# A layer norm, state-space scan and gated MLP kernel: 512-token chunks, 64-row matmul pairs for the half tiles, input constant moved to C

## Chip, cores, metric

The kernel runs on one core of a Trainium2 chip. The metric is device time in microseconds, taken from runs of the whole program; a run's profile gives its own, slightly shorter span. Engines in the profile are PE (TensorE), PEld (TensorE weight loads), DVE (VectorE), ACT (ScalarE), POOL (GpSimd) and SP (SyncE, which here issues DMAs). "L404" is line 404 of the kernel that was profiled. The granted clock is the share of TensorE's full clock that the trace records, 1.00 being full. An evacuation is the copy of a matmul's result out of TensorE's result memory.

## The reference, cut to what matters

Input x is 2048 tokens by 448 features, bf16. F is 1792, the state has 448 complex channels.

```python
xn = layernorm(x)
Lam_bar = exp(dt * Lam);  B_bar = ((Lam_bar - 1) / Lam)[:, None] * Bmat       # complex, 448 x 448
h[t] = Lam_bar * h[t-1] + B_bar @ xn[t]                                     # 2048 steps
s = 2 * Re(h @ Cmat.T) + xn * Dskip
z = (sigmoid(xn @ w_gate) * (xn @ w_up)) @ w_down
out = x + s * silu(z)
```

448 is three and a half times 128, so every contraction over features has three full 128-row tiles and a half one of 64 rows.

## The kernel before

Tokens go in eight chunks of 256. Each chunk is layer-normed and transposed, goes through gate/up (`gu`), hidden product (`hF`) and down projection, and through the state part: input projection (`bu`), rotation of each channel by its phase, a real scan over time on VectorE (one instruction for the real and one for the imaginary part), rotation back, output projection (`y`). The half tile is padded with zeros to a full one: four matmuls for each contraction of 448.

```python
TC = 256; NCH = 8; KT = 4; PT = 4
...
def emit_ffn(c, xnT):
    for ft in range(FT):                                  # 14 tiles of F
        gu = ps.tile([P, 2, TC], FP32, name="gu", bufs=2)
        for cc, wmat in enumerate((wg, wu)):
            for kt in range(KT):                          # 4 full matmuls, the last half zeros
                nc.tensor.matmul(gu[:, cc, :], lhsT=wmat[:, kt, ft * P:(ft + 1) * P], rhs=xnT[:, kt, :], ...)
        if len(pending) >= DOWN_LAG:
            down_mms(*pending.pop(0))                     # down projection of the same chunk, 4 tiles behind
        ...
        nc.vector.tensor_tensor(out=hF[:], in0=sig[:], in1=ub[:], op=ALU.mult)
...
def emit_ssm(c, xnT, K):
    for pt in range(PT):                                  # 4 tiles of state channels
        ...                                               # bu = B_bar^T xn: 8 matmuls, copied to bus by ScalarE
        nc.vector.tensor_tensor(out=ta[:], in0=bus[:], in1=cosb, op=ALU.mult)
        ...                                               # tb, z
        nc.vector.tensor_tensor_scan(out=wv[:, 0, :], data0=rb, data1=z[:, 0, :], ...)
        nc.vector.tensor_tensor_scan(out=wv[:, 1, :], data0=rb, data1=z[:, 1, :], ...)
        ...                                               # tc, td, hT; 4 matmuls into y
```

The layer norm's subtraction ran on ScalarE and its square root was ScalarE's. The scheduler of the compiler chose the order within each engine.

## Time and profile before

| | before |
|---|---|
| time, median of 3 runs | 254.73 us (254.04 to 256.77) |
| span of the profiled run | 252.6 us |
| PE, DVE, ACT busy | 84%, 83%, 59% |
| period of one 256-token chunk in the middle | 24.43 us |

The first lines of the profile's page of before: the busy time of each engine with its share of the span, and the busy tenths in 40 slices of 6.3 us each.

```profile
span 252.6 us, 4548 instructions
PE 212.4 (84%) x1616; PEld 155.4 (62%) x1616; DVE 209.0 (83%) x624; ACT 149.0 (59%) x362; POOL 5.6 (2%) x14
PE   0065996388898949999999999999999799999990
DVE  4699798699999996999789978988899799286324
```

The reader sees two engines with the same share. The slices tell them apart: from the sixteenth on PE shows nines but for one seven and the end, so TensorE sets the middle of the kernel, and the loss is in the first 100 us. Stretches of 20 us of before, with busy time and instruction count of PE, PEld, DVE, ACT and POOL, then the granted TensorE clock, the busy share of the DMA engines and the GB/s that they moved:

```profile
80.00:100.00 20.00, 15.41 (x88) 8.57 (x86) 17.86 (x57) 10.99 (x28) 0.00 (x0) 0.83 0.11 21
100.00:120.00 20.00, 19.96 (x167) 16.03 (x164) 19.33 (x58) 12.11 (x34) 0.00 (x0) 1.00 0.04 13
140.00:160.00 20.00, 19.83 (x155) 14.71 (x152) 17.45 (x51) 11.68 (x31) 0.00 (x0) 1.00 0.12 27
```

From 100 to 180 us TensorE has hardly a gap (19.8 to 20.0 of each 20 us). In that stage only less TensorE work, or faster, can help.

### The profile page before, as it was taken

The numbers are of one execution on the slowest core, as the hardware profiler recorded it, in microseconds if no ns is written. First come the engines' busy times: TensorE is split into PE (matmuls) and PEld (weight loads), VectorE is DVE, ScalarE is ACT, GpSimd is POOL, SyncE is SP. The second block draws the span as 40 slices with busy tenths as digits, with TensorE's granted clock in tenths as the row PEclk, the third lists the DMA queues.
The fourth block names the chain that finished last, engine by engine and source line by source line (L and its number), as shares of the span: only waits on it lengthen the run. The fifth ranks groups of instructions, "written<-read, shape, count | busy, mean of one in ns | idle before, by whom it ended". The sixth has DMA issues, their size and how long they took to land.

```text
span 252.6 us, 4548 instructions
## 1 busy us (share of the span) xinstructions
PE 212.4 (84%) x1616; PEld 155.4 (62%) x1616; DVE 209.0 (83%) x624; ACT 149.0 (59%) x362; POOL 5.6 (2%) x14
## 2 busy tenths in 40 slices
PE   0065996388898949999999999999999799999990
PEld 0043974275487704887688668867888377756750
DVE  4699798699999996999789978988899799286324
ACT  6595999965564527665565566547656465453331
POOL 8000000000000000000000000000000000000000
PEclk9998899799999976999999999999999999999997
DMA  6999930000211002100210021011100010001001
GB/s 215 207 301 324 313 13 3 0 0 0 25 36 21 3 0 43 38 3 0 42 39 0 3 42 36 3 22 21 39 1 3 0 35 4 0 0 40 0 0 39
DMA packets 15863, 12.07 MB, mean 48 GB/s; under 512 B 7232, under 2 KB 14912, under 8 KB 15840
## 3 DMA queue, kind: packets, MB, share of 16 engines
q1 hardware_dynamic: 15600, 11.67, 18.0%
q0 software_dynamic: 240, 0.12, 0.7%
q8 instruction: 12, 0.20, 0.3%
q14 instruction: 11, 0.09, 0.1%
HBM read 8.37 MB, written 1.84 MB: 40 GB/s over the span
## 4 chain that ended last, share of the span: by engine, by line
PE 47%; DVE 29%; ACT 10%; DMA 9%; issue 4%; SPq 1%; ACTq 0%; DVEq 0%
PE gu L390 22%; DMA wu<-in_B_w_up_dram 6%; DVE wv L352 5%; DVE wv L354 5%; PE bu L329 5%; DVE hF L404 3%; DMA b_im<-in_A_B_im_dram 3%; DVE tb L347 3%; DVE z L349 2%; DVE ta L345 2%; DVE td L366 2%; ACT bus L334 1%; ACT ct_350 L256 1%; DVE tc L364 1%; PE dacc_2979 L382 1%
## 5 line engine op out<-in xcount | busy, mean ns | idle before, releaser
L390 PE MATMUL gu<-xnT,wg 128*128 128x256 bf16 x448 | 71.4, 276 | 9.2 <-ACT ub L403 8.5
L390 PE MATMUL gu<-xnT,wu 128*128 128x256 bf16 x448 | 74.9, 276 | 1.2 <-DMA wu<-in_B_w_up_dram 1.2
L397 ACT ACTIVATE sig<-gu 128x256 bf16<-128x256 f32 x112 | 43.1, 385 | 51.2 <-PE gu L390 51.0
L390 PEld LDWEIGHTS <-wg 128*128 128x128 bf16 x448 | 44.1, 99 | 24.0 <-issue 9.9
L390 PEld LDWEIGHTS <-wu 128*128 128x128 bf16 x448 | 44.2, 99 | 7.2 <-DMA wu<-in_B_w_up_dram 1.7
L329 PE MATMUL bu<-xnT,bbarT 128*128 128x256 bf16 x256 | 46.5, 275 | 0.9 <-ACT bus L334 0.8
L403 ACT CAST ub<-gu 128x256 bf16<-128x256 f32 x98 | 36.2, 370 | 0.0
L382 PEld LDWEIGHTS <-hF 128*128 128x128 bf16 x224 | 20.7, 98 | 21.1 <-DVE hF L404 14.6
L329 PEld LDWEIGHTS <-bbarT 128*128 128x128 bf16 x256 | 25.2, 99 | 8.6 <-issue 2.9
L404 DVE TENSOR_TENSOR hF<-sig,ub 128x256 bf16<-128x256 bf16 x98 | 26.3, 280 | 4.6 <-ACT ub L403 4.4
L334 ACT CAST bus<-bu 128x512 bf16<-128x512 f32 x32 | 18.7, 590 | 12.1 <-ACT ub L403 4.7
L371 PEld LDWEIGHTS <-hT 128*128 128x128 bf16 x128 | 12.9, 102 | 13.5 <-issue 2.6
L305 ACT ACTIVATE xm<-x_all,nmean 128x448 bf16<-128x448 bf16 x16 | 9.8, 673 | 12.2 <-DVE xn L306 7.7
L345 DVE TENSOR_TENSOR ta<-bus,cosT 128x512 bf16<-128x512 bf16 x32 | 13.2, 415 | 3.9 <-ACT cosT L294 2.0
L426 DVE TENSOR_TENSOR g_t<-zb,sigd 128x448 bf16<-128x448 bf16 x16 | 6.2, 386 | 10.5 <-ACT zb L413 10.5
L368 DVE TENSOR_TENSOR hT<-tc,td 128x512 bf16<-128x512 bf16 x32 | 12.9, 416 | 1.7 <-PE y_1143 L371 1.6
L347 DVE TENSOR_TENSOR tb<-bus,spm 128x512 bf16<-128x512 bf16 x32 | 13.2, 413 | 1.2 <-ACT spm L290 1.2
L349 DVE TENSOR_TENSOR z<-ta,tb 128x512 bf16<-128x512 bf16 x32 | 13.4, 420 | 0.4
L364 DVE TENSOR_TENSOR tc<-wv,cosT 128x512 bf16<-128x512 bf16 x32 | 13.4, 419 | 0.2
L366 DVE TENSOR_TENSOR td<-wv,spm 128x512 bf16<-128x512 bf16 x32 | 13.4, 417 | 0.0
L400 DVE TENSOR_TENSOR hF<-sig,gu 128x256 bf16<-128x256 bf16 x14 | 5.9, 419 | 8.4 <-ACT sig L397 8.4
L313 PE MATMUL tpx<-ident,xn 128*128 128x128 bf16 x16 | 2.1, 311 | 12.5 <-DVE xn L306 12.4
(238 smaller groups left out, 338.7 us busy)
## 6 DMA issues: line engine op xcount, KB each, us to landing
out_dram<-o_t SPq DMA_DIRECT2D x16, 112.0 KB, 1.9
wd<-in_B_w_down_dram SPq DMA_DIRECT2D x1, 1568.0 KB, 9.1
wg<-in_B_w_gate_dram SPq DMA_DIRECT2D x1, 1344.0 KB, 11.2
wu<-in_B_w_up_dram SPq DMA_DIRECT2D x1, 1344.0 KB, 15.1
x_all<-in_A_x_dram SPq DMA_DIRECT2D x1, 1120.0 KB, 11.6
x_all<-in_A_x_dram SPq DMA_DIRECT2D x1, 672.0 KB, 4.4
c_re<-in_A_C_re_dram SPq DMA_DIRECT2D x1, 336.0 KB, 15.9
c_im<-in_A_C_im_dram SPq DMA_DIRECT2D x1, 336.0 KB, 16.2
```

The source lines that it names most:

```text
L329: nc.tensor.matmul(bu[:, cc, :], lhsT=K["bbarT"][:, kt, cc, pt * P:(pt + 1) * P], rhs=xnT[:, kt, :], start=(kt == 0), stop=(kt == KT - 1))
L334: nc.scalar.copy(out=bus[:], in_=bu[:])
L345: nc.vector.tensor_tensor(out=ta[:], in0=bus[:], in1=cosb, op=ALU.mult)
L347: nc.vector.tensor_tensor(out=tb[:], in0=swap_pair(bus[:]), in1=spm_v, op=ALU.mult)
L349: nc.vector.tensor_tensor(out=z[:], in0=ta[:], in1=tb[:], op=ALU.add)
L364: nc.vector.tensor_tensor(out=tc_[:], in0=wv[:], in1=cosb, op=ALU.mult)
L366: nc.vector.tensor_tensor(out=td[:], in0=swap_pair(wv[:]), in1=smp_v, op=ALU.mult)
L382: nc.tensor.matmul(dacc[j][:, :], lhsT=hF[:, j * P:(j + 1) * P], rhs=wd[:, ft, :], start=(ft == 0), stop=(ft == FT - 1))
L390: nc.tensor.matmul(gu[:, cc, :], lhsT=wmat[:, kt, ft * P:(ft + 1) * P], rhs=xnT[:, kt, :], start=(kt == 0), stop=(kt == KT - 1))
L397: nc.scalar.activation(sig[:], gu[:, 0, :], ACT.Sigmoid)
L403: nc.scalar.copy(out=ub[:], in_=gu[:, 1, :])
L404: nc.vector.tensor_tensor(out=hF[:], in0=sig[:], in1=ub[:], op=ALU.mult)
```

## The change

Its intent: give TensorE less to do. The half K tiles are no longer padded. Gate and up (and the real and imaginary half of the input projection) each have a 64-row half tile; the two lie in the lower and the upper 64 rows of the array and run as a pair. The last state tile holds the real part of its 64 channels in the lower and the imaginary part in the upper rows, so that seven tiles replace eight. The constant (Lam_bar − 1)/Lam is moved from B to C. Chunks are 256, 512, 512, 512, 256 tokens. Down and output projections run one chunk behind (`side_steps`). TensorE's order is written by hand. From chunk 1 on the square root becomes three Newton steps on VectorE, and the layer norm's subtraction goes to GpSimd. `P` is 128 and `H` is 64. The diff, cut to its core (most of the setup, the loads and the state part are left out):

```diff
-TC = 256
-NCH = S_TOK // TC
-KT = 4
+LMAX = 512
+CHUNKS = [(0, 2), (2, 4), (6, 4), (10, 4), (14, 2)]
+NCH = len(CHUNKS)
...
+    ctx.enter_context(tc.manual_schedule(engines={ENG.PE}))
...
+        def chain():                                   # layer norm, reciprocal square root
...
+                for _ in range(3):
+                    V.scalar_tensor_tensor(out=t, in0=y, scalar=-0.5, in1=y, op0=ALU.mult, op1=ALU.mult)
+                    V.tensor_tensor(out=t, in0=t, in1=ve, op=ALU.mult)
+                    V.scalar_tensor_tensor(out=y, in0=t, scalar=1.5, in1=y, op0=ALU.add, op1=ALU.mult)
...
+                eng = nc.gpsimd
+                eng.tensor_scalar(out=xm[:], in0=x_all[:, t0 + i, :], scalar1=nmean[:, i, :], scalar2=None, op0=ALU.add)
...
+        def do_half():
+            for i in range(nb):
+                lo = H if (i == 1 and ROWPAIR) else 0
+                nc.tensor.matmul(banks[i][:, 0:n], lhsT=halves[i], rhs=xnT[lo:lo + H, 3, 0:n],
+                                 start=half_first, stop=not half_first)
...
+    for c in range(1, NCH):
...
+        side = side_steps(c - 1)
...
+            slots = weave(npairs, (side, 0, npairs - 1), (ssm_steps(c), 0, npairs - 1))
...
+        for p in range(npairs):
+            if p == 0 and not last:
+                with tc.issue_after(anchors["hF"]):
+                    run(ln)                            # layer norm of chunk c+1
+                xnTs[c + 1] = emit_xnT(c + 1, xns[c + 1])
...
+            for k in range(2):
+                kind, cc, i = units[2 * p + k]
+                (gu_unit if kind == "gu" else bu_unit)(cc, xnTs[cc], i, k == 1)
...
+            run(slots[p])
```

Two lines of this decide the outcome. `issue_after(anchors["hF"])` holds the next chunk's layer norm back until the last hidden product of the chunk before. `weave` spreads the scans of chunk c evenly over the same loop. Both end up in VectorE's queue, whose order the scheduler then fixes.

## The prediction

> **What bounds it now.** From about 100 to 205 us one 256-token chunk takes 24.43 us (the chain of waits starts a gate/up burst at 100.41, 124.84, 149.27, 173.70). In the timeline back-to-back matmuls start every 0.109 us at 256 columns and 0.189 us at 448. A chunk's 112 gate/up, 32 input-projection, 28 down and 16 output matmuls make 15.7 + 8.3 = 24.0 us, so TensorE sets this stage. VectorE is close behind: the stretches of 20 us between 100 and 180 show it busy 17.3 to 19.3 us. The ends are worse: the first gate/up matmul starts at 15.3 us, and in 40-60 and 80-100 us TensorE is busy only 13.1 and 15.4 us. There the groups show it waiting for evacuations.
>
> **TensorE after.** Per 512 tokens, counting a 512-column matmul 0.216 us (estimate, twice 0.109): gate/up 14 x 7 = 21.2, input projection 25 x 0.216 = 5.4, down 10.6, output 28 x 0.189 = 5.3; sum 42.5 us against 48.1. This assumes that two 64-row matmuls run side by side, as the Trainium skill says (TensorE: Matmul & The Clock Gate, Part 3, "The mechanism"); the trace of before has none and can't show it. If they serialise, 46. TensorEngine Tiling (Array Packing), "Key Properties", says that a change of tiling drains the array[...]. Whole kernel: about 185 us of TensorE work (200 serialised) against 212 busy.
>
> **VectorE after.** It gets hardly less. Spacings in the timeline: bf16 tensor-tensor 0.205 us at 256, 0.34 at 512 (estimate 0.61 at 1024), scan of 256 0.66 (estimate 1.2 at 512), dependent small ones 0.15 to 0.2. Stacking saves about a seventh of the scan-and-rotate work, larger operands save fixed costs, the complex diagonal matrices and part of the table building go. But the reciprocal square root by Newton steps, the copies of xn's last columns, the stacked tile's swaps, y's direct PSUM read and the scaling of C are added. Adding the spacings over the new order gives about 206 us; the same sum on the old order gives 202, where the page shows 209 busy. So VectorE carries about 210 us, and the time is VectorE's work plus what it idles.
>
> **Stages.** Start: x comes first in small loads, first gate/up at about 11 us instead of 15.3. Chunk 0 to about 36 us, limited by VectorE and the tables on ScalarE; later weights land around 17 us, costing TensorE 2 us. Chunk 1: VectorE does two chunks' scans, the scaling of C and a layer norm, 64 us, before its last hidden tile, at about 102 us; the order puts the first five hidden products behind chunk 0's scans, so TensorE idles some 15 us around 45-60 us. Then TensorE has about 114 us left, VectorE 108: nearly balanced, ending at 216 to 219 with the tail. Mutual stalls add a few us, hidden ones of ScalarE nothing (25 us per 512 tokens).
>
> **Predicted: 220 us, 207 to 235.** Faster 0.94, same 0.04, slower 0.02.
>
> **To check.** First gate/up at 11 us; pairs of 64-row matmuls starting within some ns of each other; a long TensorE idle in 40-65 us released by VectorE's hidden product or ScalarE behind it; VectorE busy about 210 us, over 90% from 40 us on; a full 512-token chunk taking 43 to 49 us.
>
> **What would make it wrong.** Pairs that serialise (+10 us); GpSimd's subtractions and table products slow, or slowing VectorE; in-order stalls between VectorE and TensorE in the last chunks (+10); VectorE's dependent instructions overlapping better than counted (-10).

## The result, and the profile after

| | before | after |
|---|---|---|
| time, median of 4 runs each | 255.26 us (254.04 to 256.77) | 248.07 us (246.75 to 249.24) |
| ratio, 95% interval | | 0.9721 (0.9668 to 0.9774) |
| PE, DVE, ACT, POOL busy in the profile | 212.4, 209.0, 149.0, 5.6 us | 207.2, 201.9, 112.4, 38.8 us |

A ratio here and below is the mean time of one kernel's runs over that of the other's runs of the same rounds, so it is not quite the ratio of the medians. The change is faster by 2.8%; I had said 14%. The same lines as above of the page of after (slices are 6.2 us, and the third and last one is the granted TensorE clock in tenths):

```profile
span 247.4 us, 3300 instructions
PE 207.2 (84%) x1131; PEld 98.4 (40%) x1144; DVE 201.9 (82%) x540; ACT 112.4 (45%) x220; POOL 38.8 (16%) x36
PE   7199448799999999298059999999499999999980
DVE  7959998999999999999987992899975539944434
PEclk9679965599999999989758999999779999999997
```

The nines on PE now break after 99 us: slices 17 to 20 read 2, 9, 8, 0. Stretches of 20 us of after:

```profile
60.00:80.00 20.00, 19.89 (x106) 8.28 (x107) 19.86 (x41) 13.16 (x22) 0.00 (x0) 1.00 0.00 1
100.00:120.00 20.00, 12.54 (x54) 4.84 (x56) 19.88 (x60) 6.35 (x12) 7.30 (x4) 0.91 0.02 6
120.00:140.00 20.00, 13.54 (x57) 5.39 (x59) 17.40 (x39) 4.70 (x8) 0.00 (x0) 0.74 0.17 39
160.00:180.00 20.00, 16.58 (x80) 7.32 (x80) 19.53 (x62) 7.96 (x15) 2.86 (x2) 0.89 0.11 26
```

What TensorE waited for in after from 104 us to the end, the two longest (the engine's operation, what it waited for, then total, count and longest wait in us):

```profile
PE bu L419 <- DMA xnT<-xn: 12.7, 2, 9.4
PE acc L579 <- DVE hF L449: 3.5, 1, 3.5
```

The releaser is called a DMA, and that reading stops too early: the DMA transposes landed 2.4 us after issue, while the wait was 9.43 us. Four of them go out one after another, so 6.5 us pass from the first issue (119.87) to the release (126.41); but the first could not go out before `xn` was there. What was late is `xn`. (Whether another way to transpose, as TensorE does it for chunks 0 and 1, would shorten this was not tried.) VectorE's timeline of after (start, duration, engine, line, operation) shows why:

```profile
103.96 0.41 DVE L449 TENSOR_TENSOR hF<-sig,ub 128x512 bf16<-128x512 bf16 x1
104.29 1.14 DVE L166 BATCH_NORM_STATS2 stats<-x_all 128x6 f32<-128x448 bf16 x2
...
107.02 1.25 DVE L510 TENSOR_TENSOR_SCAN wv<-r_col,st_121,z 128x512 bf16<-128x512 f32 x1
...
109.53 0.53 DVE L189 TENSOR_SCALAR rs_y<-ve 128x4 int32<-128x4 int32 x1
109.97 1.27 DVE L510 TENSOR_TENSOR_SCAN wv<-r_col,st_121,z 128x512 bf16<-128x512 f32 x1
111.17 0.53 DVE L190 TENSOR_SCALAR rs_y<-rs_y 128x4 int32<-128x4 int32 x1
...
112.40 1.27 DVE L547 TENSOR_TENSOR_SCAN wv_1542<-r_col,st_123,z 128x512 bf16<-128x512 f32 x1
...
118.41 0.16 DVE L196 RECIPROCAL rsd<-sd_b 128x4 f32<-128x4 bf16 x1
...
119.07 0.57 DVE L209 TENSOR_SCALAR xn<-xm,rsd 128x448 bf16<-128x448 bf16 x2
```

The layer norm of chunk 3 begins right behind chunk 1's last hidden product (started at 103.96), and then takes 14.1 us to its `rsd` at 118.41, because each of its tiny steps stands in line behind scans and rotations of chunk 2 whose results nobody needs soon. The transposes follow on SP's queue, and TensorE, in its own fixed order, has come to the input projection of chunk 3 and stops (last column in brackets: idle before, and its releaser):

```profile
104.42 0.55 PE L579 MATMUL acc<-wd,hF 128*128 128x448 bf16 x1 [3.54 <-DVE hF L449]
...
126.41 0.61 PE L419 MATMUL bu<-xnT,bT 64*128 64x512 bf16 x2 [9.43 <-DMA xnT<-xn]
126.95 2.74 PE L413 MATMUL bu<-xnT,bT 128*128 128x512 bf16 x6
...
134.44 0.61 PE L419 MATMUL gu<-xnT,wk 64*128 64x512 bf16 x4
134.98 0.82 PE L413 MATMUL gu<-xnT,wg 128*128 128x512 bf16 x3
```

After the wait the six full matmuls take 2.74 us where six take 1.47 us elsewhere: the granted clock was 0.50 between 122.5 and 130 us. The Trainium skill (TensorE: Matmul & The Clock Gate, Part 1, "What's actually happening") says that half rate is the default and comes back after at least one idle window of about 3.4 us; this trace agrees, with 0.50 after the 9.43 us wait and 0.51 after the one of 3.54 us. The third experiment's kernel below does not: its clock was 0.50 at 113 to 116 us and at 185 to 187 us, behind waits of only 1.99 and 2.36 us.

The last two lines answer the question of the pairs. Four 64-row matmuls of 512 columns, two pairs, take 0.54 us from their start to that of the next full matmul. Four in a row would take at least 0.86.

### The profile page after: what moved, and what is told of

Read it like the earlier page. It is cut to its first block, busy times and chain, and to the rows that moved or that the text cites. A ratio compares the mean times of both kernels' runs of the same rounds, so it can differ in the third digit from the quotient of the medians.

```text
span 247.4 us, 3300 instructions
## 1 busy us (share of the span) xinstructions
PE 207.2 (84%) x1131; PEld 98.4 (40%) x1144; DVE 201.9 (82%) x540; ACT 112.4 (45%) x220; POOL 38.8 (16%) x36
## 4 chain that ended last, share of the span: by engine, by line
DVE 52%; PE 40%; issue 3%; DMA 2%; ACT 2%; POOL 0%; DVEq 0%; POOLq 0%
PE acc L579 12%; PE gu L413 12%; DVE wv L510 7%; PE acc L586 5%; PE bu L413 3%; DVE stats L166 3%; DVE hF L449 3%; PE gu L419 2%; DVE z L503 2%; DVE xn L209 2%; DVE tb L501 2%; DVE ta L499 2%; DMA xnT<-xn 2%; DVE hT L529 2%; DVE tc L525 2%
## 5 line engine op out<-in xcount | busy, mean ns | idle before, releaser
L445 ACT ACTIVATE sig<-gu 128x512 bf16<-128x512 f32 (+1 forms) x56 | 30.5, 545 | 55.0 <-PE gu L419 41.5
L579 PE MATMUL acc<-wd,hF 128*128 128x448 bf16 x224 | 49.2, 365 | 4.5 <-DVE hF L449 4.5
L413 PE MATMUL gu<-xnT,wg 128*128 128x512 bf16 (+1 forms) x200 | 47.9, 345 | 1.9 <-issue 0.9
L413 PE MATMUL gu<-xnT,wu 128*128 128x512 bf16 (+1 forms) x208 | 49.1, 345 | 0.2
L208 POOL TENSOR_SCALAR xm<-x_all,nmean 128x448 bf16<-128x448 bf16 x14 | 22.4, 1617 | 119.6 <-issue 117.4
L413 PEld LDWEIGHTS <-wu 128*128 128x128 bf16 x210 | 21.2, 101 | 17.1 <-issue 1.7
L413 PEld LDWEIGHTS <-wg 128*128 128x128 bf16 x210 | 17.8, 100 | 23.1 <-issue 12.7
L413 PE MATMUL bu<-xnT,bT 128*128 128x512 bf16 (+1 forms) x104 | 25.7, 388 | 0.7 <-ACT bus_598 L469 0.7
L449 DVE TENSOR_TENSOR hF<-sig,ub 128x512 bf16<-128x512 bf16 x42 | 17.0, 413 | 10.2 <-ACT ub L448 10.1
L448 ACT CAST ub<-gu 128x512 bf16<-128x512 f32 x42 | 24.4, 580 | 0.0
L586 PE MATMUL acc<-cT,hT 128*128 128x448 bf16 x98 | 21.7, 363 | 0.0
## 6 DMA issues: line engine op xcount, KB each, us to landing
wu<-in_B_w_up_dram SPq DMA_DIRECT2D x1, 960.0 KB, 11.1
```

The source lines that it names most:

```text
L208: eng.tensor_scalar(out=xm[:], in0=x_all[:, t0 + i, :], scalar1=nmean[:, i, :], scalar2=None, op0=ALU.add)
L413: nc.tensor.matmul(banks[i][:, 0:n], lhsT=fulls[i](kt), rhs=xnT[:, kt, 0:n], start=(kt == 0 and not half_first), stop=(kt == KF - 1 and ha ...
L445: nc.scalar.activation(sig[:, 0:n], gu[:, 0, 0:n], ACT.Sigmoid)
L448: nc.scalar.copy(out=ub[:, 0:n], in_=gu[:, 1, 0:n])
L449: anchors["hF"] = nc.vector.tensor_tensor(out=hF, in0=sig[:, 0:n], in1=ub[:, 0:n], op=ALU.mult).ins
L579: nc.tensor.matmul(dacc[:, 0:D], lhsT=hFs[c][:, ft, j * P:(j + 1) * P], rhs=wd[:, ft, :], start=(ft == 0), stop=(ft == FT - 1))
```

## The experiments

Each kernel was timed in 3 rounds against before on the same chip; before's medians were 254.5 to 254.8 us. After was not timed again in these rounds, so a difference to it, or between kernels of separate rounds, is one of medians of separate rounds; the ratios to before, each within its own rounds, are the fairer comparison. "Theory A" in the first texts is that the next layer norm comes too late in VectorE's order. In kernels where the subtraction was moved, line numbers from L208 on are one lower.

### Half of the cure: start the layer norm earlier

```diff
-                with tc.issue_after(anchors["hF"]):
-                    run(ln)
+                if c == 1:
+                    with tc.issue_after(anchors["hF"]):
+                        run(ln)
...
+            if p == npairs // 2 and c + 2 < NCH:
+                with tc.issue_after(anchors["hF"]):
+                    run(ln_steps(c + 2))
```

> The layer norm of chunks 3 and 4 is ordered half a chunk earlier on VectorE; nothing else. Theory A (TensorE loses about 20 us because the next chunk's normalised tile comes late: 9.4 + 3.3 us of waiting and about 5.5 us at half clock behind it): the two waits for the transposing transfers vanish, about 230 us. Rival B (VectorE is full until about 127 us, so work put in front pushes the last hidden products of chunk 1 back): the wait for the transfer vanishes but the wait of 3.5 us for the hidden product grows to about 10 us; 241 to 246 us. Rival C (GpSimd shares a resource with VectorE and that is what costs): no change, 247 to 249 us.

Measured: 238.27 us (236.49 to 239.05), ratio to before 0.9359 (0.9313 to 0.9405). Neither theory A's 230 us nor rival B's 241 to 246 came out. The wait for `xnT` is gone from TensorE's list. In its place stand longer waits for VectorE, as B had foreseen in kind:

```profile
PE acc L579 <- DVE hF L449: 6.3, 3, 4.1
PE acc L586 <- DVE s_t L601: 3.7, 1, 3.7
```

So the late layer norm is a cause (about 10 us), and starting it half a chunk earlier pushes other urgent work back.

### Hold the scans behind the hidden products

```diff
+        ssm_c = ssm_steps(c) if c > 1 else []
...
+        if c > 1:
+            def gated(f, a=anchors["hF"]):
+                with tc.issue_after(a):
+                    f()
+            slots = [[(lambda f=f: gated(f)) if f in ssm_c else f for f in sl] for sl in slots]
```

> Scan steps of chunks 2 to 4 may not be ordered ahead of the last hidden product of the chunk before; the layer norm stays where it was relative to that product. B: the 12 us of chunk 2's scans that stood ahead of chunk 1's last hidden product move behind it, that product comes at about 91 instead of 104 us, TensorE no longer waits for it, and the wait for the transfer shrinks to about 5 us: 236 to 240 us. A alone (only the layer norm's place counts): the norm also comes 12 us earlier, so a gain too, about 235 us; the pair of waits in the trace tells them apart. C: no change.

Measured: 241.77 us (239.18 to 242.02), ratio 0.9483 (0.9429 to 0.9537). The hidden-product wait of after (3.5 us) is gone, but the transposed tile is as late as ever:

```profile
PE bu L419 <- DMA xnT<-xn: 12.7, 2, 9.3
```

The scans and the layer norm now became free at the same moment, and the scheduler interleaved them again: from the first statistics of chunk 3 at 96.27 us to its `rsd` at 110.88 are 14.6 us, as long as in after. Both texts missed: chunk 1's last hidden product came at 95.93 us and not at 91, and the wait for the transfer did not shrink.

### Hold the scans behind the next layer norm

The same gate, on another instruction: the last copy of the next chunk's `xn`. No work is added or taken away.

```diff
-            V.tensor_copy(out=xn[:, i, 448:512], in_=xn[:, i, 384:448])
+            anchors["ln"] = V.tensor_copy(out=xn[:, i, 448:512], in_=xn[:, i, 384:448]).ins
...
-            def gated(f, a=anchors["hF"]):
-                with tc.issue_after(a):
+            def gated(f):
+                with tc.issue_after(anchors["ln"]):
```

> As the run before, and the scan steps also stand behind the layer norm of the next chunk. Neither A nor B leaves a cause for TensorE to wait between 95 and 180 us: both waits and the half-clock stretches behind them go, 20 us in all, so 226 to 231 us, TensorE busy without a gap from about 50 us to the end. If VectorE's amount of work (not its order) is the limit, 240 us or more, with the wait moved to the output matmuls waiting for the rotated state. C: 247 us.

Measured: 232.78 us (232.22 to 234.05), ratio 0.916 (0.9121 to 0.9198). This is 15.3 us less than after, with the same instructions on VectorE. The expected 226 to 231 us were missed by 2. Chunk 3's statistics start at 96.33 and `rsd` comes at 103.38, 7.1 us instead of 14.1, and TensorE's wait of 9.43 us shrinks to 1.99:

```profile
96.33 1.15 DVE L166 BATCH_NORM_STATS2 stats<-x_all 128x6 f32<-128x448 bf16 x2
103.38 0.18 DVE L196 RECIPROCAL rsd<-sd_b 128x4 f32<-128x4 bf16 x1
111.62 0.39 PE L419 MATMUL bu<-xnT,bT 64*128 64x512 bf16 x2 [1.99 <-DMA xnT<-xn]
```

The stretches of this kernel that answer to those of after:

```profile
100.00:120.00 20.00, 18.01 (x84) 7.31 (x84) 19.44 (x49) 7.95 (x15) 5.58 (x4) 0.91 0.15 32
120.00:140.00 20.00, 20.00 (x102) 8.46 (x101) 18.26 (x39) 11.48 (x21) 0.00 (x0) 1.00 0.04 13
160.00:180.00 20.00, 20.00 (x113) 9.13 (x110) 19.93 (x42) 10.02 (x20) 0.00 (x0) 1.00 0.02 7
```

VectorE's column hardly differs from after's (19.88, 17.40, 19.53). TensorE's is 18.01, 20.00 and 20.00 instead of 12.54, 13.54 and 16.58. What changed is what VectorE did first. Of the 15.3 us, 6.3 are the second experiment's, where the hidden product came earlier; 9.0 come with the layer norm in front. Through the ratios to before (0.9721 and 0.916) the 15.3 are 14.3 us.

### Take the subtraction off GpSimd

```diff
-                eng = nc.gpsimd
-                eng.tensor_scalar(out=xm[:], in0=x_all[:, t0 + i, :], scalar1=nmean[:, i, :], scalar2=None, op0=ALU.add)
+                nc.scalar.activation(xm[:], x_all[:, t0 + i, :], ACT.Identity, bias=nmean[:, i, :])
```

> The mean is subtracted on ScalarE (about 0.67 us each, as in the kernel before) instead of on GpSimd (1.6 us each). C (GpSimd at work stretches small VectorE instructions from 0.15 to about 0.53 us in 109 to 116 us): VectorE saves 2 to 3 us in each of the three stretches, 241 to 244 us, and the stretched instructions vanish. A and B: the norm's chain is ordered as before and ends at most 2 us earlier, 245 to 248 us.

Measured: 244.43 us (243.32 to 244.98), ratio 0.9596 (0.9557 to 0.9636): 3.6 us less than after. The Trainium skill (SBUF — State Buffer, "Who interferes with whom") says that GpSimd shares VectorE's second pair of ports and that, where both need it (for VectorE: two SBUF inputs, or some copies, casts and `tensor_scalar`), whoever issues first has it for its whole instruction and the other fully blocks. The time lies between the two expectations (241 to 244 and 245 to 248 us). The trace of after agrees that there is blocking: with four GpSimd subtractions running from 109.03 to 116.33 us, exactly four small VectorE instructions are stretched, from about 0.16 to 0.48 to 0.53 us. The size is less clear: a GpSimd subtraction lasts 1.62 us on average over the run, the four stretches are all near 0.36 us, which what remains of a whole instruction would hardly be each time. GpSimd may have been the loser too: these four took 7.30 us, and chunk 1's four, at 25.55 us, 5.58 us (GpSimd's spans are rough). The same instruction without GpSimd, in this kernel:

```profile
107.82 0.17 DVE L189 TENSOR_SCALAR rs_y<-ve 128x4 int32<-128x4 int32 x1
```

The four stretches are 1.5 us in this layer norm, and VectorE's busy time falls by 5.2 us in all (201.9 to 196.7) with as many instructions; how much of the 3.6 us is this and how much the different order that the scheduler then chose is not settled.

### Both cures together

The gate of the third experiment and the ScalarE subtraction of the fourth.

> The layer norm first (as in the run of that name, 232.8 us) and the mean subtracted on ScalarE. If the two causes, the late tile and GpSimd's company, are separate, the 3.6 us that the second gave alone come on top for the most part: 229 to 231 us. If moving off GpSimd helped only because the tile came earlier, which is now no longer waited for, 232 to 234 us.

Measured: 229.41 us (228.25 to 230.39), ratio 0.9017 (0.8983 to 0.905). It is correct and beats both kernels, 18.7 us below after. The two gains add up: 15.3 and 3.6 make 18.9 (through the ratios, 14.3 and 3.2 against 17.9). Run again on another chip:

> The same kernel as the best one so far, run again on this chip so that the next two have it beside them. Every theory: 229.4 us within 1 us.

Measured: 228.73 us (228.24 to 229.74), ratio 0.8993 (0.8946 to 0.9041). Its stretches from 60 us on have TensorE at 19.7 to 19.9 of 20 us up to 160:

```profile
80.00:100.00 20.00, 19.90 (x101) 8.19 (x101) 19.37 (x56) 12.94 (x24) 0.00 (x0) 1.00 0.04 12
100.00:120.00 20.00, 19.80 (x101) 8.45 (x102) 19.73 (x44) 10.72 (x20) 0.00 (x0) 1.00 0.17 33
140.00:160.00 20.00, 19.68 (x105) 8.84 (x105) 19.46 (x56) 11.05 (x22) 0.00 (x0) 1.00 0.11 26
```

The repeat run's trace shows what GpSimd's company cost in the third experiment's kernel. Chunk 3's layer norm stands in the same order on VectorE in both; from the first statistics to the last copy of `xn` it takes 8.0 us here and 10.1 there, and the wait of 1.99 us for `xnT` is gone. The difference lies in instructions that were stretched there. The same one, there and here:

```profile
102.79 0.56 DVE L195 TENSOR_TENSOR sd_b<-rs_y,ve 128x4 bf16<-128x4 f32 x1
```

```profile
99.94 0.16 DVE L195 TENSOR_TENSOR sd_b<-rs_y,ve 128x4 bf16<-128x4 f32 x1
```

### Are the 64-row pairs worth it?

The third experiment's kernel with both halves of every pair in the lower 64 rows, so that they must run one after the other. The result is wrong on purpose (relative error 0.33): the upper operands are replaced by the lower ones.

```diff
-ROWPAIR = True
+ROWPAIR = False
...
-                 ... (wk[0:H, fs], wk[H:P, fs]), half_first)
+                 ... (wk[0:H, fs], wk[0:H, fs]), half_first)
...
-                 [bT[(H if i else 0):(P if i else H), 3, m * P:(m + 1) * P] for i, m in enumerate(ms)], half_first)
+                 [bT[0:H, 3, m * P:(m + 1) * P] for i, m in enumerate(ms)], half_first)
```

> Wrong result on purpose: the second half tile uses the first half's rows of weights and tokens, so that the two 64-row matmuls of a pair share array rows; base is the run with the layer norm first (232.8 us). If the pairs run side by side (four of them took 0.54 us, two pairs), about 51 pairs of 512 and 34 of 256 columns now cost one more matmul each, 14.7 us of TensorE: 243 to 247 us. If the pair saves nothing, 232 to 234 us.

Measured: 238.11 us (237.96 to 238.2), ratio 0.9345 (0.9331 to 0.9359); 5.3 us more than the kernel it is built on. First after, then this kernel, at the same place of chunk 1, a gate/up half tile followed by one of the input projection:

```profile
61.96 0.39 PE L419 MATMUL gu<-xnT,wk 64*128 64x512 bf16 x2
62.19 0.38 PE L419 MATMUL bu<-xnT,bT 64*128 64x512 bf16 x2
```

```profile
61.39 0.60 PE L419 MATMUL gu<-xnT,wk 64*128 64x512 bf16 x2
61.84 0.59 PE L419 MATMUL bu<-xnT,bT 64*128 64x512 bf16 x2
```

Two in different rows take 0.23 us to the next start, two in the same rows 0.45. So the pairs run side by side, as the Trainium skill says (TensorE: Matmul & The Clock Gate, Part 3, "The mechanism"). TensorE was busy 9.8 us longer (214.3 against 204.5), where I had counted 14.7; at full clock, reckoned as in the table further down but in steps of 1 us, it is 12.6 (207.6 against 195.0). The time rose by only 5.3: the 2.0 us wait for `xnT` and the 2.4 us wait for `s_t` of the third experiment's kernel are gone from this one's list. Here about 4.4 us of the added work filled waits, and my expectation of 10 us or more was a miss.

### Are the 512-token chunks worth it?

The third experiment's kernel with eight chunks of 256 tokens.

```diff
-LMAX = 512
-CHUNKS = [(0, 2), (2, 4), (6, 4), (10, 4), (14, 2)]
+LMAX = 256
+CHUNKS = [(2 * i, 2) for i in range(8)]
...
```

The lines left out fit the tables at the chunks' edges to the one length.

> All chunks 256 tokens instead of 512, else as the run with the layer norm first. TensorE's columns stay the same. VectorE has twice as many instructions: about 0.07 to 0.1 us more for each of some 150 more, and the norm's chain eight times instead of five, 15 to 25 us more in all; if VectorE's amount still counts, 242 to 255 us; if only TensorE counts, 232 to 236 us.

Measured: 248.87 us (247.28 to 250.08), ratio 0.9764 (0.9722 to 0.9806), 16.1 us more than the third experiment's kernel, and so close to before that the verdict at 2% is unclear. VectorE is busy 217.7 us instead of 202.7 with 761 instructions instead of 540, and TensorE waits for the transposed tile five times:

```profile
PE bu L419 <- DMA xnT<-xn: 13.5, 5, 4.3
```

The longer chunks save fixed costs on VectorE. How the 16 us split between the work and these waits was not taken apart.

### What keeps the rest of the way to 220 us?

First guess: the slow start is a cold TensorE clock. Throw-away matmuls of 512 columns were put before the transposes and setup matmuls of chunks 0 and 1.

```diff
+    def fill(n):
+        g = ps.tile([P, 2, 512], FP32, name="gu", bufs=2)
+        for _ in range(n):
+            nc.tensor.matmul(g[:, 0, :], lhsT=warm[:, 0:P], rhs=warm[:], start=True, stop=True)
...
+                fill((12 if c == 0 else 10) if j == 0 else 3)
```

> As the run before, with throw-away matmuls put where TensorE waits between 6 and 48 us, so that its clock is not halved at 33 to 46 us and at 10 to 15 us. If the start of chunk 1 waits for TensorE's slow matmuls there, 3 to 5 us less than the run before. If VectorE and ScalarE set that stretch, no change, or up to 1 us more.

Measured: 233.93 us (233.44 to 235.24), ratio 0.9189 (0.9159 to 0.922), 4.5 us slower. The clock was 1.00 at 8 to 16 us (0.50 to 0.74 without the fillers) and 0.80 to 1.00 at 32 to 48 us, but the fillers stood in front of the transposes; the first 512-column gate/up of chunk 1 came at 49.5 us instead of 44.9. The guess is not supported, and the test was a poor one: in the trace of the best kernel the clock had been 1.00 from 32 to 44 us anyhow (the half clock at 33 to 46 us is after's).

Second guess: TensorE's own order holds chunk 1's gate/up back behind the input projection of chunk 0. They were interleaved; the buffers allowed it only with all of C's scaling right behind the fifth gate/up unit (two earlier forms deadlocked when built). A second kernel has only that move of the scaling.

```diff
     for pt in range(4):
-        bu_unit(0, xnTs[0], pt, pt % 2 == 1)
+        bu_unit(0, xnTs[0], pt, False)
+        gu_unit(1, xnTs[1], pt, True)
...
-            slots = weave(npairs, (c_steps(), 0, 3), ...
+            slots = weave(npairs, (c_steps(), 0, 0), ...
```

> On top of the best kernel: the first four gate/up units of chunk 1 run between the four input-projection units of chunk 0, instead of behind them, and all of C's scaling is put behind the fifth unit. It asks where the last 9 us to the predicted 220 are. In the best kernel TensorE is busy 20.0 of 20 us almost without a break from 60 to 160 us but only 13.6 in 20-40 and 18.1 in 40-60, and chunk 1's first gate/up comes at 44.9 us where I had predicted 36. Theory 1 (the late start is TensorE waiting in its own order for the input projection's copies, and TensorE is the limit afterwards): first 512-column gate/up at about 39 us and 225 us or less. Theory 2 (VectorE, busy over 19 of 20 us from 15 to 160 us, is the limit, and TensorE only catches up with it): the gate/up moves forward, the wait reappears before a hidden product or a scan, and the time stays at 228 to 231 us.

> The best kernel with only the second half of the former edit: all of C's scaling behind the first pair of units of chunk 1 instead of spread over four pairs. It separates the two halves of that edit. Both theories: within 1.5 us of the best kernel (228 to 231 us). If it alone gains 3 us or more, the early gate/up units are not what a gain of the former run comes from.

Measured: 235.9 us (235.46 to 236.32), ratio 0.927 (0.9224 to 0.9316), for both edits; 236.67 us (235.48 to 237.34), ratio 0.9299 (0.9237 to 0.9362), for the scaling alone. The early gate/up came at 39.91 us as planned and gained 0.8 us, within the spread. The wait came back a little later, in the first of these lines; the second is of the kernel with the scaling alone:

```profile
PE tpc L390 <- DVE cT L399: 9.2, 2, 6.8
```

```profile
PE tpc L390 <- DVE cT L399: 4.9, 2, 3.7
```

Theory 1 is refused for this edit: TensorE started sooner and only waited sooner, for VectorE. Theory 2 had the returning wait right, but not the time (228 to 231 us). The scaling alone was a miss: I had expected nothing within 1.5 us and it cost 7.9. From 60 to 80 us VectorE is busy 15.29 us in it, where the best kernel has 19.90; that kernel's line comes second. VectorE here waited for ScalarE's copies of the up half before hidden products (7.6 us in all). I read this as TensorE standing at the scaling's transposes, so that the copies came late; the time that VectorE stood idle in this stage was not made up later.

```profile
60.00:80.00 20.00, 19.73 (x94) 7.57 (x94) 15.29 (x29) 10.93 (x19) 0.00 (x0) 0.95 0.00 1
```

```profile
60.00:80.00 20.00, 19.89 (x104) 8.41 (x106) 19.90 (x39) 13.18 (x22) 0.00 (x0) 1.00 0.00 1
```

## Why the prediction was wrong

The step that failed is the sentence "Mutual stalls add a few us". The sum that I made was: last hidden product of chunk 1 at 102 us, 114 us of TensorE work after it, and about 4 us for stalls and tail. The trace of after has, term by term:

| term | predicted | measured in after | difference |
|---|---|---|---|
| last hidden product of chunk 1 (VectorE's timeline) | 102 | 103.96 | +2 |
| TensorE busy from 104 to 241 us, at full clock | 114 | 122.2 less 6.8 = 115.4 | +1 |
| of it lost to reduced clock (busy time times one minus the granted clock, in steps of 2 us) | 0 | 6.8 | +7 |
| TensorE idle from 104 to 241 us (137.0 less 122.2) | few, with the tail 4 | 14.8 | +15 |
| last matmul to the end (241 to 247.4) | in the 4 | 6.4 | +2 |

The differences make 27 us, which is the distance from 220 to the span of 247.4. The idle and the reduced clock that follows it are 22 of them.

- **Right: the work.** TensorE's work after the milestone (chunk 1's last hidden product) was 115.4 us against 114; over the whole kernel it was 192.2 us at full clock (207.2 busy less 15.0) against about 185. In the best kernel (the second run), where the clock is full from 44 us to the last matmul, a whole 512-token chunk takes 44.35 us from one input projection at 108.55 us to the next at 152.90; I had said 43 to 49. VectorE was busy 201.9 us against a sum of 206 and an estimate of 210.
- **Right: the pairs.** They run side by side, 0.23 us against 0.45 for a pair. About 0.1 us goes with a change of tiling, which I had guessed without a measurement: in after two gate/up units, from 133.05 to 136.29 us, take 3.24 us with two changes, where fourteen matmul slots of 0.216 us are 3.02.
- **Right by luck, two errors cancelling: the start.** First gate/up at 12.4 us (said 11). I had chunk 1 start at 36 and TensorE idle for 15 us at 45 to 60. In after chunk 1's first gate/up came at 47.9, and there was no such idle. Both errors vanish in the milestone, because VectorE, busy 99% of the time from 40 to 100 us, sets it. That VectorE would be over 90% busy "from 40 us on" held only to 120 us: it was 14.2 of 20 us at 140 to 160 and 11.1 at 180 to 200.
- **Wrong: the wait.** I listed "in-order stalls between VectorE and TensorE in the last chunks (+10)" as a way to be wrong, but gave the prediction no share of it. I counted VectorE's total and didn't ask in which order it works. The order in the built kernel was there to be read: the layer norm of the next chunk behind the last hidden product, and its eighteen small, mostly dependent steps woven in between scans. With both engines near full, the time here depended on which piece of VectorE's work came first. The reordering alone, with no change of work, gave 15.3 of the 28 us; this is shown by the third experiment, and the second shows that the gate must be on the layer norm and not on the hidden product.
- **Wrong: GpSimd.** I named "GpSimd's subtractions and table products slow, or slowing VectorE" as a risk without a size. Moving the subtraction gave 3.6 us alone and 3.4 on top of the reordering. There some 2 us of stretched VectorE instructions, on the path that TensorE waited for, match the wait of 1.99 us that went away; the rest was not traced.
- **Open: the last 9 us.** The best kernel is at 229, inside the range of 207 to 235 but not at 220. TensorE's waits after 160 us (waits for `hF` 3.2 and `s_t` 2.5 us in all in its profile) and a tail of about 6 us stand against about 4 us forecast for both; what the start adds was not taken apart. An early gate/up was tried only with an edit that cost 7.9 us by itself, and gained 0.8 us beside it; whether a different order in the last two chunks would gain was not tried.

Where the expected gain went is thus named: 7 us came through at once, 19 were turned into a new wait of TensorE for VectorE's order, with the clock that it lost by waiting, and into what the subtraction on GpSimd cost; those 19 came back with two small edits.

## What to carry to other kernels

When two engines are nearly equally busy (here 84 and 82%), add up not only what each has to do but what each has to do first: follow the one item that the other engine will stop for (here the next chunk's normalised, transposed input), and count what stands before it in the queue. Give the scheduler that order explicitly; a gate that frees urgent and unurgent work at the same moment left the layer norm as slow as before here (14.6 against 14.1 us). When the profile names a DMA as the releaser of a long wait, compare its landing time with the wait, and if it is much shorter, go on to what the DMA waited for.

## What the Trainium skill lacked or had wrong

- TensorE: Matmul & The Clock Gate, Part 1, "What's actually happening": the half clock is said to come back after at least one idle window of about 3.4 us. In the third experiment's kernel it came behind waits of only 1.99 and 2.36 us; in the best kernel's repeat, waits of 1.63 and 1.68 us left the clock full.
- SBUF — State Buffer, "Who interferes with whom": a VectorE instruction with two SBUF inputs is said to contend with a GpSimd instruction that reads SBUF, and the later one to block for the whole of the other. Here four small VectorE instructions, two of them with one input, grew by about 0.36 us each beside GpSimd instructions of 1.62 us on average; the other 17 that started in that stretch (109.1 to 116.2 us) grew by 0.04 us at most, among them products of two SBUF tiles of 128x512, which took 0.41 to 0.42 us as elsewhere.
- GPSIMD Engine Reference, "4.1 Engine selection": one-input elementwise work on GpSimd is called roughly line-rate. Here a one-input subtraction of 128x448 bf16 took 1.62 us on GpSimd (spans there are rough); in the kernel before the same one took 0.67 us on ScalarE, and a one-input product of that size (L306) 0.33 us on VectorE.
- TensorEngine Tiling (Array Packing), "Key Properties": a change of tiling is said to drain the array, and no cost is given. Here about 0.1 us went with a change.
- Perfetto Trace Analysis, "Identifying the Most-Contended Engine": the engine with the highest occupancy is to be optimised first, TensorE being judged by MFU and by the busy share of its weight loads. In after the weight loads took 40% (PEld) and VectorE 82%, but 15.3 us came from the order of VectorE's work alone, with its busy time hardly changed (201.9 and 202.7 us). Following the gaps, as the page's next section says, led there.
- No page gives the time of a DMA transpose of a 128x512 bf16 tile within SBUF (VectorE: DVE Perf Modes, "The three transpose paths", has one of 128x128 alone): here 1.2 us to issue on SP's queue and 2.4 us to land, so four in a row took 5.1 us to issue.
